# Keeping the intermediate rows of a Fourier mixing kernel in SBUF instead of DRAM, on one Trainium2 core

## The chip, the core and the metric

The kernel runs on one core of one Trainium2 chip. The metric is the device time of one execution in microseconds (us). Every execution quoted here is of the fast state, so no comparison in this document mixes states. The profile is one execution of the same program, with its own span. Engines are called TensorE (PE in the profile, its weight loads PEld), VectorE (DVE), ScalarE (ACT), GpSimd (POOL) and SyncE (SP).

## The reference, cut to what matters

```python
def _attn_ref(x, filt_r, filt_i):                 # x (8, 3136, 256): eight entries
    X = np.fft.rfft(x, axis=1)                    # along the 3136 rows
    Y = X * (filt_r + 1j * filt_i)[None, :, :]
    return np.fft.irfft(Y, n=x.shape[1], axis=1)

def _moe_ref(x, w_in, w_out, g_ln):               # x (25088, 256)
    h = x @ w_in                                  # 256 -> 1024
    e = np.exp(h - max(h));  sm = e / (sum(e) + 1e-09)
    solu = h * sm
    ln = (solu - mean(solu)) / sqrt(var(solu) + 1e-06) * g_ln
    return ln @ w_out                             # 1024 -> 256
```

The transform is done as matrix products of two lengths, 49 and 64 (3136 = 49 x 64): first products `pa` over 49, then per frequency a product `pb` over 64, the filter, the inverse product `pc` over 64, and products `py` back over 49. The second part works in 196 blocks of 128 rows: product `h`, maximum, exponential, normalization, a transposition through SBUF and DMA, product `po`. A block needs the rows of one entry (24.5 blocks each), so the entries 2 to 7 can be transformed beside the blocks of their forerunners.

## The kernel before

Between `pa` and `pb`, and between `pc` and `py`, rows and columns have to change places between partitions. The kernel before does this by a round trip through DRAM each time. Its entries go in groups: entries 0 and 1 together before any block (the prologue), then four groups spread over 150 blocks.

```python
GROUPS = [((0, 1), None, None),                   # prologue
          ((2,), (0, 6), (9, 13)),                # first blocks of pa; of pb/pc
          ((3, 4), (6, 13), (22, 25)),
          ((5, 6), (32, 28), (64, 29)),
          ((7,), (94, 18), (116, 24))]
...
    def store_first(self, i, dma):                # t1 (after pa) -> DRAM
        b, ch = divmod(i, NH // NCH)
        dma(out=d1[self.n][b].rearrange("a (h n) c -> (a h) n c", h=2)[
            :, NCH * ch:NCH * ch + NCH, :], in_=self.t1s.pop(i))

    def fetch(self, i):                           # DRAM -> t2: two DMAs, 64 partitions each
        ...
        for p in range(2):
            nc.sync.dma_start(out=self.t2s[i][N2 * p:N2 * p + N2, 0:cols, :],
                              in_=self.rows(d1[self.n], s, count, p))

    def store(self, i, dma):                      # g (after pc) -> DRAM: two DMAs
        ...
def fetch_back(e, ch, rows_pool):                 # DRAM -> t4, before py
    ...
# in the loop over blocks k:
    hidden(k)          # 8 passes h, 512 columns
    turn(k - 1); regroup(k - 4)       # four DMAs on SyncE
    early jobs         # pa, pb, py of later entries
    project(k - 6)     # 16 passes po, 256 columns
    normalize(k); scale(k - 6)
    products, late jobs, stores, loads
```

The cuts are marked by "..." and by the comments that stand for code.

## Time and profile before

| | before |
|---|---|
| time, median of 3 | 1903.86 us (1903.44 to 1904.51) |
| TensorE busy | 96 % |
| first product `h` in the trace | 203.4 us |
| HBM read, written | 118.44 MB, 81.40 MB |

The chain that ended last follows the work back from the end of the execution. The first line splits it by engine, the second by engine, operation and source line. From the page of the kernel before:

```profile
PE 88%; DVE 4%; DMA 2%; issue 1%; ACT 1%; POOL 0%; ACTq 0%; DVEq 0%; SPq 0%; POOLq 0%
PE h L396 35%; PE po L456 35%; PE py L253 6%; PE pc L226 4%; PE pb L196 4%; PE pa L169 3%; DMA d<-t 1%; DVE p L217 1%; DVE i L216 0%; DVE p L215 0%; DVE g L229 0%; DMA t<-d 0%; DVE nmax L401 0%; DMA f<-f_dram 0%; DMA raw_in<-in_moe_w_in_dram 0%
```

TensorE carries 88 % of the time, 70 % in the two products of the blocks. All round trips through DRAM together hold 1 % of the chain (`d<-t` and `t<-d`), though they are a large part of the 200 MB that pass through HBM: nearly nothing waits for them.

### The profile page before, as it was taken

The page shows a single profiled execution, that of the slowest core. Times are in us where ns is not written, and L with a number is a line of the kernel's source. Part 1 is how long each engine was busy: PE and PEld are TensorE (multiplying, and loading weights), DVE is VectorE, ACT ScalarE, POOL GpSimd, SP SyncE. Part 2 cuts the span into 40 slices and gives each one's busy share as a digit, 9 for nine tenths or more (in the row PEclk, how much of TensorE's full clock was granted, in tenths as well). Part 3 has the DMA queues.
Part 4 walks back from the last instruction along what each step waited for, and adds up shares of the span by engine and source line. Part 5 has one row for each costly group of instructions (what it writes and reads, how often), then busy time and mean ns, then how long its engine had stood idle before and what let it go on. Part 6 is the DMA issues. An engine that isn't in the chain of part 4 may idle for free.

```text
span 1902.9 us, 21234 instructions
## 1 busy us (share of the span) xinstructions
PE 1823.8 (96%) x6500; PEld 1168.5 (61%) x6500; DVE 1137.0 (60%) x1815; ACT 791.5 (42%) x1297; POOL 440.7 (23%) x1293
## 2 busy tenths in 40 slices
PE   6677889999999999999999999999999999999997
PEld 1224546676666666666666666667677676666665
DVE  1597445567766655566766655566666565566663
ACT  1142344554555544444545434344444334333331
POOL 2010133343334311123333211123322010110110
PEclk9686799999999999999999999999999999999999
DMA  9675279986877866575776656557675545434444
GB/s 268 214 211 188 92 226 239 241 209 174 189 194 204 200 150 149 134 170 140 166 186 148 151 137 141 137 134 177 146 178 112 119 100 117 99 86 110 96 92 100
DMA packets 320399, 300.78 MB, mean 158 GB/s; under 512 B 28625, under 2 KB 286418, under 8 KB 320288
## 3 DMA queue, kind: packets, MB, share of 16 engines
q1 hardware_dynamic: 284624, 206.69, 46.3%
q0 software_dynamic: 26704, 79.63, 14.9%
q10 hardware_dynamic: 8960, 13.11, 2.3%
q8 instruction: 53, 0.87, 0.2%
q14 instruction: 58, 0.48, 0.1%
HBM read 118.44 MB, written 81.40 MB: 105 GB/s over the span
## 4 chain that ended last, share of the span: by engine, by line
PE 88%; DVE 4%; DMA 2%; issue 1%; ACT 1%; POOL 0%; ACTq 0%; DVEq 0%; SPq 0%; POOLq 0%
PE h L396 35%; PE po L456 35%; PE py L253 6%; PE pc L226 4%; PE pb L196 4%; PE pa L169 3%; DMA d<-t 1%; DVE p L217 1%; DVE i L216 0%; DVE p L215 0%; DVE g L229 0%; DMA t<-d 0%; DVE nmax L401 0%; DMA f<-f_dram 0%; DMA raw_in<-in_moe_w_in_dram 0%
## 5 line engine op out<-in xcount | busy, mean ns | idle before, releaser
L456 PE MATMUL po<-w_out_sb,solu_t 128*128 128x256 f32 x3136 | 711.0, 380 | 4.5 <-DVE ot L464 4.5
L396 PE MATMUL h<-w_in_sb,y 128*128 128x512 f32 x1568 | 713.4, 598 | 0.0
L456 PEld LDWEIGHTS po<-w_out_sb,solu_t 128*128 128x128 f32 x3136 | 591.0, 190 | 137.7 <-issue 58.1
L396 PEld LDWEIGHTS h<-w_in_sb,y 128*128 128x128 f32 x1568 | 296.2, 192 | 317.8 <-issue 306.7
L401 DVE TENSOR_REDUCE nmax<-h 128x1 f32<-128x1024 f32 x196 | 239.6, 1222 | 419.6 <-PE h L396 419.6
L404 ACT ACTIVATE e<-h,nmax 128x1024 f32<-128x1024 f32 x196 | 218.5, 1115 | 605.0 <-DVE nmax L401 605.0
L421 ACT ACTIVATE e<-solu,nmu 128x1024 f32<-128x1024 f32 x196 | 225.0, 1148 | 287.9 <-DVE solu L419 287.9
L419 DVE SCALAR_TENSOR_TENSOR solu<-e,rsum,h 128x1024 f32<-128x1024 f32 x196 | 250.9, 1280 | 7.1 <-DVE rsum L416 0.2
L429 DVE STREAM_TRANSPOSE turn<-solu 128x1024 f32<-128x1024 f32 x196 | 241.8, 1234 | 0.0
L235 POOL DMA_DIRECT2D d<-g x152 | 93.7, 621 | 507.5 <-ACT g L229 507.4
L253 PEld LDWEIGHTS py<-wi_t,t 100*128 100x128 f32 x1024 | 146.0, 211 | 51.1 <-issue 36.0
L169 PE MATMUL pa<-x,wf_t 98*100 98x512 f32 x256 | 148.5, 687 | 25.9 <-DMA x<-in_x_dram 12.5
L253 PE MATMUL py<-wi_t,t 100*128 100x98 f32 x1024 | 145.4, 293 | 6.7 <-DMA t<-d 3.5
L448 POOL COPY rs_t<-rs 32x1 f32<-32x1 f32 x784 | 141.7, 181 | 35.7
L464 DVE TENSOR_SCALAR ot<-po,rs_t 128x256 f32<-128x256 f32 x196 | 94.4, 482 | 80.5 <-PE po L456 74.2
L215 DVE TENSOR_TENSOR p<-pb,f 128x512 f32<-128x512 f32 (+1 forms) x101 | 69.0, 684 | 120.4 <-ACT i L208 119.3
L196 PE MATMUL pb<-t,de 128*128 128x512 f32 (+1 forms) x250 | 110.9, 544 | 19.2 <-DVE p L215 10.0
L226 PE MATMUL pc<-p,de 128*128 128x512 f32 (+1 forms) x250 | 110.0, 539 | 14.9 <-DVE p L217 11.5
L442 POOL TENSOR_SCALAR rs<-var 128x4 f32<-128x4 f32 x49 | 9.3, 189 | 445.7 <-ACT e L421 443.6
L169 PEld LDWEIGHTS pa<-x,wf_t 98*100 98x100 f32 x256 | 45.7, 188 | 94.5 <-issue 59.9
L196 PEld LDWEIGHTS pb<-t,de 128*128 128x128 f32 x250 | 47.8, 198 | 78.4 <-issue 43.5
L256 ACT COPY y<-py 128x392 f32<-128x392 f32 x112 | 93.6, 836 | 5.1 <-PE py L253 5.1
(62 smaller groups left out, 868.2 us busy)
## 6 DMA issues: line engine op xcount, KB each, us to landing
solu_t<-turn SPq DMA_DIRECT2D x784, 128.0 KB
t<-d SPq DMA_DIRECT2D x64, 400.0 KB
t<-d SPq DMA_DIRECT2D x198, 128.0 KB
x<-in_x_dram SPq DMA_DIRECT2D x64, 392.0 KB
out_dram<-ot SPq DMA_DIRECT2D x196, 128.0 KB
d<-t POOLq DMA_DIRECT2D x48, 400.0 KB, 5.6
d<-g POOLq DMA_DIRECT2D x148, 128.0 KB, 3.6
f<-f_dram POOLq DMA_DIRECT2D x104, 128.0 KB, 4.3
```

What stands on the lines that cost most here:

```text
L169: nc.tensor.matmul(out=ps[0:NK, j], lhsT=wf_t, rhs=self.xs[i][0:NR, 2 * u:2 * u + 2, :], start=True, stop=True)
L196: nc.tensor.matmul(out=ps[:, w * j:w * j + w, :], lhsT=de[:, s + j, 0, :], rhs=t2[:, w * j:w * j + w, :], start=True, stop=True)
L226: nc.tensor.matmul(out=ps[:, w * j:w * j + w, :], lhsT=de[:, s + j, 1, :], rhs=pt[:, w * j:w * j + w, :], start=True, stop=True)
L253: nc.tensor.matmul(out=psv[:, i, :], lhsT=t4s[e, ch][:, i, cb * P:cb * P + P], rhs=wi_t, start=True, stop=True)
L396: nc.tensor.matmul(out=h[:, half, :], lhsT=y[:, c, P * t:P * t + P], rhs=w_in_sb[:, c, 512 * half:512 * half + 512], start=(c == 0), stop= ...
L401: nc.vector.tensor_reduce(out=nmax, in_=h, axis=AX.X, op=ALU.max, negate=True)
L404: nc.scalar.activation(out=e, in_=h, func=AFT.Exp, bias=nmax, accum_out=esum)
L419: nc.vector.scalar_tensor_tensor(out=solu, in0=e, scalar=rsum, in1=hs.pop(k), op0=ALU.mult, op1=ALU.mult, accum_out=nmu)
L421: nc.scalar.activation(out=e, in_=solu, func=AFT.Square, bias=nmu, scale=-float(DFF), accum_out=variances[g][:, i:i + 1])
L429: nc.vector.transpose(out=turns[g][:, :, i, :], in_=solus.pop(k).rearrange("p (f j) -> p f j", j=32))
L448: nc.gpsimd.tensor_copy(out=rss[g][32 * i:32 * i + 32, c:c + 1], in_=rs[32 * c:32 * c + 32, i:i + 1])
L456: nc.tensor.matmul(out=ps, lhsT=solu_t[:, f, :], rhs=w_out_sb[:, f, :], start=(f == 0), stop=(f == KF - 1))
```

## The change

Its intent is to drop the round trips. After `pa` the rows of one entry lie in one SBUF tile, `rows` (100 partitions x 32 x 256). A frequency is then one partition of it, 32 KB, and has to be spread over 32 partitions for `pb`; after `pc` the 32 partitions are gathered into the one, in place. Each such move is one DMA of 32 KB: four of each kind for one column of the transform, eight each way for a unit of two. Because there is one tile, the entries can only follow one another: entry 0 alone before the blocks, entry e beside the 24.5 blocks of entry e-1. To make room, the eviction buffer `g` has one buffer beside the blocks instead of two.

```diff
-    d1 = [dram.tile([len(g[0]), 2 * NS, N2, C], FP32, ...) for n, g in enumerate(GROUPS)]
-    d2 = [dram.tile([len(g[0]), 2 * NS, N2, C], FP32, ...) for n, g in enumerate(GROUPS)]
+    rows = consts.tile([P, NH, C], FP32, name="rows")
 ...
+        def first(self, i, kind, evac):
+            ps = psum(kind, f"pa_{self.e}_{i}")
+            nc.tensor.matmul(out=ps[0:NK], lhsT=wf_t, rhs=self.xs.pop(i)[0:NR], ...)
+            evac(out=rows[0:NK, 2 * i:2 * i + 2, :], in_=ps[0:NK])
+
+        def fetch(self, i):
+            for j in range(count):
+                for a in range(4):
+                    r = NS * a + s + j
+                    nc.sync.dma_start(out=self.t2s[i][NH * a:NH * a + NH, j, :], in_=rows[r:r + 1])
 ...
+        def store(self, i, dmas):
+            for j in range(count):
+                for a in range(4):
+                    r = NS * a + s + j
+                    dmas[a](out=rows[r:r + 1], in_=gt[NH * a:NH * a + NH, j, :])
+
+        def back(self, i, kind, evac):            # py reads rows directly
 ...
-        for name, bufs in (("r", 4), ("t1", 2), ("t2", 3), ("p", 2), ("g", 2))}
+        for name, bufs in (("r", 5), ("i", 1), ("p", 2), ("g", 1))}
 ...
+    for e in range(1, B):
+        base = S * (e - 1) // P
+        pa   at blocks base      to base + 4
+        pb   at blocks base + 6  to base + 18, one unit a block; pc one block later
+        py   at blocks base + 20 to base + 23
```

The last four lines stand for the longer code of the schedule. Weights are unpacked elsewhere in the prologue, and the filter is copied once and saved to DRAM from SBUF.

> **What bounds the kernel now.** I read the page's busy shares first, then its 40 slices, then the stage table, because an average over stages hides where the change acts. On the page, the busy shares, the slices and the costliest groups:
>
> ```profile
> PE 1823.8 (96%) x6500; PEld 1168.5 (61%) x6500; DVE 1137.0 (60%) x1815; ACT 791.5 (42%) x1297; POOL 440.7 (23%) x1293
> ...
> PE   6677889999999999999999999999999999999997
> ...
> DVE  1597445567766655566766655566666565566663
> ...
> PEclk9686799999999999999999999999999999999999
> DMA  9675279986877866575776656557675545434444
> ...
> L456 PE MATMUL po<-w_out_sb,solu_t 128*128 128x256 f32 x3136 | 711.0, 380 | 4.5 <-DVE ot L464 4.5
> L396 PE MATMUL h<-w_in_sb,y 128*128 128x512 f32 x1568 | 713.4, 598 | 0.0
> ```
>
> The reader sees two kernels in one. In the first five slices (47.6 us each) TensorE is busy 6 to 8 tenths and its clock is 0.6 to 0.9; after that TensorE is full. The stage table (time, TensorE, weight load, VectorE, ScalarE, GpSimd busy, granted clock, DMA share, GB/s) says the same in numbers:
>
> ```profile
> 100.00:150.00 50.00, 36.00 (x62) 11.30 (x62) 47.72 (x82) 21.06 (x36) 3.60 (x6) 0.90 0.67 195
> 150.00:200.00 50.00, 38.19 (x136) 29.39 (x137) 30.25 (x60) 10.51 (x15) 2.14 (x3) 0.60 0.49 161
> ...
> 400.00:600.00 200.00, 200.00 (x721) 128.49 (x720) 131.80 (x208) 101.42 (x169) 69.77 (x176) 1.00 0.78 192
> ```
>
> From 100 to 150 us VectorE is the bound (47.7 of 50). From 400 us TensorE is busy for every microsecond at clock 1.00 and VectorE has a third to spare. The timeline shows the first block matmul (h) at 203.4 us. So the kernel is a **prologue** of 204 us (entries 0 and 1 through the transform, weights unpacked, nothing else for TensorE) and a **block stage** of 1699 us (196 blocks of h and po, the other six entries beside them).
>
> What does a unit of TensorE work cost? A busy duration is not it, since matmuls overlap. The chain of waits between 389 and 404 us, where nothing waits, gives it:
>
> ```profile
> 391.49 0.87 PE py L253 x8
> ...
> 397.56 0.95 PE py L253 x8
> 398.51 3.46 PE h L396 x8
> 401.97 0.86 PE pb L196 x4
> 402.83 0.86 PE pa L169 x2
> 403.69 3.45 PE po L456 x16
> ```
>
> So a pass of 512 columns takes 0.43 us, one of 256 columns 0.216, one py pass 0.109. Check: between 500 and 1700 us the trace has 1140 h, 2272 po, 96 pa, 88 + 50 pc, 86 + 50 pb (512 and 256 columns) and 736 py passes: 490.2 + 490.8 + 41.3 + 48.6 + 47.8 + 80.2 = 1198.9 of 1200 us. The block stage runs at the array's rate.
>
> **What the Trainium skill says.** (1) "TensorE: Matmul & The Clock Gate", Part 1 (The HAM clock gate): the array runs at half clock until it has been busy for some 3.4 us. The prologue's 0.60 to 0.90 against 1.00 later agrees. A prologue made of waits is paid twice. (2) "DMA: Bandwidth & Descriptors", Issuing engines are not separate DMA queues: transfers from all issuers share 16 engines, and several issuers save issue time only. Here an issue on SyncE or ScalarE costs 0.28 to 0.62 us (medians 0.28 for a store of t1 on ScalarE, 0.43 for an output, 0.62 for a 64-partition load), one on GpSimd 0.61. (3) "SBUF — State Buffer", Door 1 (The DMA port swizzle): four partitions share a port and reached 27.6 GB/s alone. A 32 KB row sits in one partition, so an estimate from that page is 32.8 KB / 27.6 GB/s = 1.2 us per row move unless rows on different ports overlap. No transfer of the kernel before has this shape, so nothing in its trace tests it.
>
> **The change part by part.** The intermediate goes from two DRAM round trips to one resident tile, rows. Each row (one frequency, 32 x 256) is moved from its partition to 32 partitions by one DMA, and put back by another: 200 row moves of 32 KB per entry. Entry 0 alone is in the prologue; entries 1 to 7 each take the 24.5 blocks before they are needed.
>
> *Block stage, TensorE.* One entry needs 32 pa passes (13.8), 100 pb/pc passes of 256 columns (21.6) and 128 py passes (14.0): 49.3 us. Before: 196 x (8 x 0.43 + 16 x 0.216) = 1351.6, plus 6 x 49.3 = 295.8, sum 1647; the stage took 1699, so 52 us are lost. The table's idle and the tail (1850 to 1903 us holds 42.9 busy of 53) put about 10 at the end, and some 42 between 204 and 400, where the clock is 0.76 and 0.86 at first and the chain waits for DMA d<-t and f<-f_dram. After: 1351.6 + 7 x 49.3 + 3.5 (ps_mean moves here) = **1700 us**. So the seventh entry costs 49 us in the stage that was full. Weight loads grow (800 instead of 500 for pb and pc) but at 256 columns they hide, as they do for po.
>
> *Prologue.* It halves in work, and what bounds it changes. The first landing is at 5.4 us in the trace. x of one entry (3.2 MB) with the tables and two raw weights queued beside it (3.6 MB) at the 250 GB/s or so of the first slices: about 28 us. Then VectorE: one unit is three operations started every 0.605 us (1.8); a weight unpacking is ten operations of 0.42 or 0.69, some 5.1 us in a row; a filter copy is 2 x 0.95. Before the first product stand two unpackings and two copies (14 us), partly under the x load, and the first row needs about 6 us of issue and landing: first product near 40 us. The 13 units with two unpackings and three copies make 23.6 + 10.2 + 5.7 = 40 us on VectorE. SyncE issues ten row moves per unit: at 0.3 us that is 39 us for 13 units, at 0.6 it is 78. I take 45 to 50 for the phase, so its products end near 88. Last inverse, put-back and landing: 5 to 6 us. The 16 back pieces are 14 us at full clock, some 18 with a cold start, beside four unpackings (20 us) on VectorE. Blocks start near **115 us** by this (88 + 6 + 18 = 112, and 3 for what queues behind the tables) instead of 204.
>
> *Startup and tail.* Blocks 0 to 4 now have 2.75 us of pa beside 3.44 of h, so TensorE is less empty than before; but entry 1's x may land only after the pools of the prologue are free, behind the 3.3 MB that saves the filters. I take 15 us of losses instead of 42, partly for the seven seams between entries (pb of the first unit two blocks after its rows are fetched). The tail is untouched: 10 us.
>
> *Beside it.* A unit block has 8.6 us of TensorE work. VectorE needs 4.7 + 2.05, GpSimd eight put-backs at 0.61 plus two filter loads (1.2) and 1.1 of scale work, 7.2; SyncE eight row fetches, four regroups at 0.62 and its share of output, 5.3 at 0.3 us per row and 7.7 at 0.6. All fit, GpSimd and SyncE narrowly. DRAM traffic falls.
>
> Sum: 115 + 1700 + 15 + 10 = **1840 us**, 3.4% less. The gain is the prologue's 89 and about 27 of startup, less 49 + 3.5 of added matmul.
>
> **The rivals.** *A: row moves serialize on the port.* At 1.2 us each, 16 per unit block are 19 us against 8.6 of TensorE, some 10 us x 13 x 7 = 900 us more; at an effective 0.6 us, with other traffic, 1 to 3 us a block and 100 to 250 us more: 1950 or worse. For it: the page's port figure. Against it: the four rows of one frequency lie 25 partitions apart, in different ports, and transfers overlap; the code has been arranged around eight row moves per block, which somebody would not keep at such a price. *B: SyncE or the outstanding transfers bound the prologue.* Issue at 0.6 us, or every DMA waiting for the eighth before it on its semaphore at 4 us under load, makes the unit phase 70 us: 1865 in all. *C: VectorE is late.* Unpacking of w_out stands ahead of the first maximum; if the raw words come late, blocks start 10 us later: 1850. *D: seams.* If SyncE or GpSimd runs behind, a regroup queues behind eight fetches that wait for a row, and po waits: 5 us x 7 entries, 1870. *E: the transfers were hidden anyway.* True from 400 us on, so the DRAM savings are worth nothing there; I give them no time.
>
> **Range and chances.** Start of blocks between 98 and 145 us, startup and seams between 8 and 35, give 1816 to 1890; 8 in 10 falls in 1815 to 1882. The 2% mark is 1866. Faster 0.77; the same 0.14 (B and D together); slower 0.09 (A).
>
> **What would show it.** The first h in the timeline, at 115 us by me. In the stage table, 200.0 of 200 TensorE at clock 1.00 through the middle; less, with a wait of pb for row fetches, is A or D. The idle of py before its first piece tells the put-back. SyncE's issue durations decide 0.3 against 0.6. From first h to the end I expect about 1725 us. The prediction is wrong most likely if row moves are slower than every transfer that the trace shows.

## The result

| | before | after |
|---|---|---|
| time, median of 4 | 1904.18 us (1903.44 to 1904.84) | 2067.31 us (2061.34 to 2074.40) |
| ratio of fast runs, 95 % interval | | 1.0858 (1.0813 to 1.0903) |
| HBM read, written | 118.44, 81.40 MB | 82.40, 28.97 MB |
| first `h` | 203.4 us | 187.2 us |

The changed kernel is correct, moves 88 MB less through HBM, and is 8.6 % slower. Ratios here and below are the mean time of one kernel's fast runs over the mean of the other's fast runs of the same rounds, so not quite the ratio of the medians.

The page of the changed kernel: busy shares, two rows of the 40 slices (51.8 us each), the chain by engine and by line, and groups (busy us, mean ns of one | idle time before them and what ended most of it).

```profile
PE 1878.0 (91%) x6800; PEld 1254.7 (61%) x6800; DVE 1114.2 (54%) x1787; ACT 824.7 (40%) x1354; POOL 700.6 (34%) x1853
...
PE   6549899899989999899999999799998999999998
...
PEclk9966999899999999899999999999999999999999
...
PE 52%; DMA 21%; SPq 9%; issue 8%; POOL 5%; DVE 2%; ACT 2%; POOLq 0%; DVEq 0%; ACTq 0%
...
L206 POOL DMA_DIRECT2D rows<-g x750 | 376.5, 505 | 351.3 <-ACT g L198 304.6
...
L174 PE MATMUL pb<-r_t,de 128*128 128x256 f32 x400 | 130.4, 435 | 96.0 <-DMA r_t<-rows 44.2
L214 PE MATMUL py<-wi_t,rows 100*128 100x98 f32 x1024 | 151.2, 315 | 49.3 <-DMA rows<-g 49.3
...
L198 ACT COPY g<-pc 128x512 f32<-128x512 f32 (+1 forms) x104 | 59.2, 569 | 255.1 <-DMA rows<-g 171.9
```

TensorE fell from 96 to 91 % busy and from 88 to 52 % of the chain. In its place stand DMA (21 %), SyncE's issues (SPq, 9 %) and GpSimd (5 %). TensorE's row has 8s and one 7 among the 9s behind the prologue, where the kernel before had only 9s until its last slice. The group lines name the waits: the evictions of `pc` (`g<-pc`) waited 171.9 us for put-backs (`rows<-g`) to land, `py` 49.3 us for the same, `pb` 44.2 us for row fetches. A wait of ScalarE for a put-back is by itself harmless; it delays the next `pc` and whatever stands behind the eviction in ScalarE's queue. Which wait of TensorE each delay ends in, the trace doesn't tell one by one: behind the first `h`, TensorE waited 40.0 us with `py` for put-backs, 22.2 with `pb` for row fetches, 16.1 with `pb` for the filter products, 14.2 with `pa` for rows of x and 8.3 with `po`.

The stage table of the changed kernel (stretch, its length, busy time of TensorE, weight loads, VectorE, ScalarE, GpSimd, granted TensorE clock, DMA share, GB/s):

```profile
50.00:100.00 50.00, 24.44 (x48) 13.90 (x48) 18.21 (x28) 9.63 (x17) 12.99 (x22) 1.00 0.67 98
100.00:150.00 50.00, 23.08 (x52) 14.24 (x52) 28.25 (x49) 12.54 (x23) 18.73 (x35) 0.65 0.54 78
150.00:200.00 50.00, 46.69 (x174) 36.73 (x175) 21.36 (x45) 20.86 (x29) 1.67 (x3) 0.63 0.49 138
400.00:600.00 200.00, 192.78 (x686) 126.21 (x686) 117.68 (x187) 85.29 (x144) 82.59 (x211) 0.99 0.74 145
1000.00:1200.00 200.00, 186.23 (x696) 126.17 (x695) 102.96 (x162) 82.89 (x136) 68.53 (x185) 0.96 0.67 129
```

From 50 to 150 us no engine is busy for more than 28 of 50 us, and 78 to 98 GB/s flow where the kernel before had 195 to 212: none of these engines is the bound by its busy time. SyncE is not in the table, since issuing a DMA doesn't count as busy: by the durations of its issues it spent 72 % of these 100 us issuing (31 % in the kernel before). The clock of 1.00 from 50 to 100 us is no measurement, since the profile's clock records begin at 98 us; at 86 us a pass of 256 columns took 0.43 us, twice the 0.216 of later ones. From 1000 to 1200 TensorE has 186 of 200 us, with a clock of 0.96, where it had 200 of 200 at 1.00.

**The balance.** I split both traces into three parts: the time to the first `h`; the TensorE work behind it, each pass priced at its undisturbed step (0.43 us for 512 columns, 0.216 for 256, 0.109 for `py`, as the prediction read them); and the rest of the time to the last product, which I call losses. Both end some 5.6 us after the last product.

| us, from the trace | first `h` | TensorE work behind it | losses |
|---|---|---|---|
| before | 203.4 | 1661.9 | 31.9 |
| after | 187.2 | 1696.8 | 181.6 |
| difference | -16.2 | +34.9 | +149.7 |
| the prediction's difference | -89 | +53 | -27 |

The sum of the differences is 168 us, as is the difference of the two spans (2071.1 and 1902.9). Two terms went wrong, the prologue by 73 us and the losses by 177.

**The circle in the prologue.** Timeline of SyncE's queue, after:

```profile
92.30 6.51 SPq L164 DMA_DIRECT2D r_t<-rows  x8
98.91 1.17 SPq L206 DMA_DIRECT2D rows<-g  x2
```

One unit costs SyncE eight fetches in 6.51 us and two of its eight put-backs in 1.17 (in the prologue GpSimd issues four and ScalarE two), 7.7 in all; one of these eight fetches lasted 1.94 us. Over the prologue the fetches start every 0.634 us in the median. Thirteen units took from 52 to 148 us, 7.4 each. From the chain of waits of the same kernel, the end of the prologue:

```profile
149.72 3.29 DMA rows<-g
153.01 0.30 issue
153.31 27.59 PE py L214 x128
180.91 6.41 PE pa L154 x8
187.32 3.43 PE h L393 x8
```

The back transform waits for the last put-back to land, and then takes 27.59 us, 0.216 a pass, twice the 0.109 of later passes: the granted clock is 0.50.

**The circle in the blocks.** Timelines of GpSimd and then of ScalarE in one stretch of a unit phase (start us, us, engine, line, operation, count, and the idle time before with what ended it):

```profile
833.25 3.99 POOL L206 DMA_DIRECT2D rows<-g  x8 [2.82 <-ACT g L198]
841.66 3.96 POOL L206 DMA_DIRECT2D rows<-g  x8 [4.42 <-ACT g L198]
```

```profile
832.38 0.58 ACT L198 COPY g<-pc 128x512 f32<-128x512 f32 x1 [2.47 <-DMA rows<-g]
840.79 0.58 ACT L198 COPY g<-pc 128x512 f32<-128x512 f32 x1 [2.58 <-DMA rows<-g]
```

ScalarE evicts a `pc` at 832.38, GpSimd issues its eight put-backs from 833.25 to 837.24, and ScalarE, idle for 2.58 us, begins the next eviction at 840.79, when the last of them has landed: `g` has one buffer. Over all unit phases the medians of one round are 0.58 us for the eviction, 0.29 to the first issue, 4.02 for eight issues, 3.77 from there to the last landing and 0.22 to the next eviction, 8.9 in all; the median from one eviction to the next is 9.16, the mean 9.71. A unit block has 8.6 us of TensorE work. In 54 of 84 rounds the next eviction began within 0.3 us of the last landing. The seam between two entries, in TensorE's timeline:

```profile
846.31 3.62 PE L453 MATMUL po<-w_out_sb,solu_t 128*128 128x256 f32 x16
856.13 5.41 PE L214 MATMUL py<-wi_t,rows 100*128 100x98 f32 x24 [6.21 <-DMA rows<-g]
```

TensorE stands still for 6.21 us until the last put-back of the entry has landed. The seams between entries cost 41 us in all, and passes of `py` and `po` that waited for nothing lost another 34 to a lower granted clock.

### The profile page after: what moved, and what is told of

The parts are those of the page before. It is cut to its first block, busy times and chain, and to the rows that moved or that the text cites. A ratio compares the mean times of both kernels' runs of the same rounds, so it can differ in the third digit from the quotient of the medians.

```text
span 2071.1 us, 24728 instructions
## 1 busy us (share of the span) xinstructions
PE 1878.0 (91%) x6800; PEld 1254.7 (61%) x6800; DVE 1114.2 (54%) x1787; ACT 824.7 (40%) x1354; POOL 700.6 (34%) x1853
## 3 DMA queue, kind: packets, MB, share of 16 engines
HBM read 82.40 MB, written 28.97 MB: 54 GB/s over the span
## 4 chain that ended last, share of the span: by engine, by line
PE 52%; DMA 21%; SPq 9%; issue 8%; POOL 5%; DVE 2%; ACT 2%; POOLq 0%; DVEq 0%; ACTq 0%
PE po L453 20%; PE h L393 18%; PE py L214 7%; DMA rows<-g 6%; DMA solu_t<-turn 5%; SPq L164 5%; DMA r_t<-rows 5%; PE pa L154 4%; POOL rows L206 4%; DMA r_x<-in_x_dram 4%; SPq L435 3%; PE pb L174 1%; DMA out_dram<-ot 1%; PE pc L195 1%; SPq L466 1%
## 5 line engine op out<-in xcount | busy, mean ns | idle before, releaser
L453 PE MATMUL po<-w_out_sb,solu_t 128*128 128x256 f32 x3136 | 726.4, 386 | 8.3 <-DVE ot L461 8.3
L453 PEld LDWEIGHTS po<-w_out_sb,solu_t 128*128 128x128 f32 x3136 | 605.4, 194 | 131.2 <-issue 35.0
L206 POOL DMA_DIRECT2D rows<-g x750 | 376.5, 505 | 351.3 <-ACT g L198 304.6
L174 PE MATMUL pb<-r_t,de 128*128 128x256 f32 x400 | 130.4, 435 | 96.0 <-DMA r_t<-rows 44.2
L214 PE MATMUL py<-wi_t,rows 100*128 100x98 f32 x1024 | 151.2, 315 | 49.3 <-DMA rows<-g 49.3
L214 PEld LDWEIGHTS py<-wi_t,rows 100*128 100x128 f32 x1024 | 150.3, 230 | 63.7 <-issue 49.2
L174 PEld LDWEIGHTS pb<-r_t,de 128*128 128x128 f32 x400 | 73.4, 205 | 180.3 <-issue 131.5
L154 PE MATMUL pa<-r_x,wf_t 98*100 98x512 f32 x256 | 142.2, 672 | 29.8 <-DMA r_x<-in_x_dram 28.9
L198 ACT COPY g<-pc 128x512 f32<-128x512 f32 (+1 forms) x104 | 59.2, 569 | 255.1 <-DMA rows<-g 171.9
L381 POOL DMA_DIRECT2D f<-f_dram x182 | 94.6, 525 | 181.6 <-DVE i L187 128.3
```

Source lines behind the costliest of these rows:

```text
L154: nc.tensor.matmul(out=ps[0:NK], lhsT=wf_t, rhs=self.xs.pop(i)[0:NR], start=True, stop=True)
L174: nc.tensor.matmul(out=ps[:, j, :], lhsT=de[:, s + j, 0, :], rhs=t2[:, j, :], start=True, stop=True)
L206: dmas[a](out=rows[r:r + 1], in_=gt[NH * a:NH * a + NH, j, :])
L214: nc.tensor.matmul(out=psv[:, j, :], lhsT=rows[0:NK, 4 * n + j, cb * P:cb * P + P], rhs=wi_t, start=True, stop=True)
L453: nc.tensor.matmul(out=ps, lhsT=solu_t[:, f, :], rhs=w_out_sb[:, f, :], start=(f == 0), stop=(f == KF - 1))
```

## The experiments

The questions were: are the row moves slow because a row lies in one partition (P, the port); because there are so many issues on SyncE (S); because the put-backs go round with one buffer (G); or does the order of entries lose by itself (O)? Kernels said to be wrong give a wrong result on purpose. Times are medians; the kernel before had 1904 to 1908 us in the same rounds.

### One fetch per row, but from a table (control): getrow, wrong

```diff
 def fetch(self, i):
+    if self.e:       # source: one partition of the constant table, 32 rows by a broadcast
+        nc.sync.dma_start(out=self.t2s[i][NH*a:NH*a+NH, j, :], in_=de[r:r+1, s, :, :] ... broadcast)
```

> Control of the run before: eight fetches per unit, each reading 32 KB from one partition of the constant table (wrong result on purpose). It differs from the changed kernel only in that a fetch no longer waits for the rows of its own entry. All theories expect no more than 20 to 30 us off 2067; what it gains is the price of the fetch waiting for the first transform at each entry's start.

Measured: 2068.33 us, ratio 1.0844 (1.0822 to 1.0865); losses 171 us. It equals the changed kernel, so the fetches' dependence on the first transform costs nothing, and the two runs below can be compared with it.

### The same eight fetches from 32 partitions each: get32, wrong

```diff
+    nc.sync.dma_start(out=self.t2s[i][NH*a:NH*a+NH, j, :], in_=de[NH*a:NH*a+NH, s + j, :, :])
```

> The row fetches stay eight per unit and 32 KB each, but each reads 32 partitions of a constant table instead of one partition (wrong result on purpose). S expects the time of the next run (eight fetches from one partition of the same table) within 15 us, since the number of issues is the same. P expects it 40 us or more faster than the next run. G expects both the same as the changed kernel, 2067, within 20.

Measured: 2104.62 us, ratio 1.1029 (1.1006 to 1.1053). With a source spread over 32 partitions it is slower, not faster. So P, the rival that I feared most, falls for the fetches. For put-backs into one partition no run here tells it. The median landing of the put-backs rose from 4.0 (getrow) to 4.8 us, and the time rose with it: the first sign that the put-backs carry the time.

### One fetch of 256 KB per unit instead of eight of 32: flatget, wrong

```diff
+    nc.sync.dma_start(out=self.t2s[i][:, 0:count, :], in_=de[:, s:s + count, :, :] ...)
```

> For entries 1 to 7 the eight row fetches of a unit (32 KB each) become one transfer of the same 256 KB, from 128 partitions of a constant table (wrong result on purpose). S (SyncE's issues bound a unit block: 8 x 0.63 + 4 x 0.70 + 0.75 = 9.2 us against 8.6 of TensorE) expects SyncE at about 5 us per unit block and 60 to 100 us off the changed kernel's 2067, to about 1985. G (the put-back chain bounds it: one g buffer, 4.0 us of GpSimd issue, then some 4 us to landing, then the next eviction) expects at most 20 us off. P (one partition's port serializes the row moves) expects some 40 to 80 off, since half of the row moves go.

Measured: 2086.84 us, ratio 1.0941 (1.0919 to 1.0964). SyncE lost seven of its eight fetch issues per unit, and the kernel got some 20 us slower (18.5 against the control getrow of the same rounds). S alone is not the bound. The put-backs landed in 4.44 us instead of 4.19, and the evictions waited 218 us for them instead of 172.

### The order alone, with the DRAM round trips of before: neworder, correct

```diff
-GROUPS = [((0, 1), None, None), ((2,), (0, 6), (9, 13)), ((3, 4), (6, 13), (22, 25)), ...]
+STARTS = [0, 0] + [S * (e - 1) // P - 10 for e in range(2, B)]
+GROUPS = [((0,), None, None)] + [
+    ((e,), (STARTS[e], 5), (STARTS[e] + (6 if e == 1 else 8), 13)) for e in range(1, B)]
 ...      # the blocks of py and how early rows are loaded follow
```

From entry 2 on, this schedule starts `pa` ten blocks and `pb` eight blocks earlier than the changed kernel does: it is the one-by-one order, but not block for block the changed kernel's.

> One part alone: the kernel before, its DRAM round trips and its few large transfers, but one entry in the prologue and entries 1 to 7 one after another beside the blocks (correct result). If the row moves are what costs (S, G or P), TensorE is full from the first blocks on, the prologue ends near 130 to 145 us and the total is 1700 + 140 + 25 + 10, about 1875, faster than both kernels. If the order itself costs (an entry's stages too dense for 24.5 blocks), it is at 1950 or above like the changed kernel.

Measured: 1957.06 us, ratio 1.0262 (1.0244 to 1.0280). First `h` at 161.9 us, 41.5 earlier than before; work behind it +36; losses 90 instead of 32. So this order costs 49 us against the kernel before in the same rounds (52 between the profiled spans) without any row move: halving the entries of the prologue doesn't halve its time, and what moves into the blocks is paid in full. Its stage table, two stretches:

```profile
350.00:400.00 50.00, 36.04 (x139) 25.52 (x138) 18.15 (x30) 14.40 (x23) 9.39 (x27) 0.83 0.58 131
...
600.00:800.00 200.00, 200.00 (x777) 138.56 (x776) 121.42 (x194) 92.55 (x152) 58.70 (x165) 0.99 0.71 174
```

Between 600 and 800 us it loses nothing; entry 1, started late and squeezed beside the first blocks, loses up to 14 of 50 us at 350 to 400.

### Two buffers for the evicted rows: g2, correct

```diff
-    ones = consts.tile(...); w_bar = consts.tile(...)      # moved into a spare buffer of g, for room
-    (("r", NB), ("i", 1), ("p", 2), ("g", 1))
+    (("r", NB), ("i", 1), ("p", 2), ("g", 2))
```

> The changed kernel with two g buffers instead of one (the two small constants of the weight preparation lie in that pool, for space; correct result). G (one put-back must land before the next eviction, and ScalarE stands still meanwhile: 172 us of its waits) expects ScalarE's wait on put-backs to fall below 60 us and 30 to 90 us off the changed kernel's 2067. S (SyncE's 9.2 us of issues per unit block) expects less than 15 us off, since SyncE's queue is as long as before. Both together in series: 15 to 40 off now, the rest in the next run but one.

Measured: 2027.39 us, ratio 1.0633 (1.0599 to 1.0667), losses 140. G is real: one more buffer gives 40 us. What is left has changed its name. The waits of TensorE in this run (total us, times, longest):

```profile
PE pb L172 <- DMA r_t<-rows: 69.6, 41, 5.6
...
PE py L212 <- DMA rows<-g: 20.1, 5, 12.4
```

`py`'s wait fell from 49.3 to 20.1 us, and `pb`'s wait for row fetches rose from 44.2 to 69.6. SyncE's steps in the block stage say why: eight fetches at 0.73 us, four regroups at 0.71 and its share of output at about 0.5 make 9.2 us per unit block, against 8.6 of TensorE. These are steps from start to start and hold waits: the issues themselves fill 76 % of SyncE's time in the unit phases of g2.

### Both at once: flatget_g2, wrong

The edits of flatget and g2 together.

> Two g buffers and one row fetch per unit from a constant table instead of eight (wrong result on purpose). If S and G are two queues of nearly the same length that hide each other, this is the first run that gains much: unit blocks at TensorE's 8.6 us, losses of the block stage from 182 to about 80 (the seven seams with their 40 us stay), 1950 to 1980 in all. If G alone counts, it equals the run with two g buffers within 15.

Measured: 1978.72 us, ratio 1.0387 (1.0356 to 1.0418), losses 85.

| us | eight fetches | one fetch |
|---|---|---|
| one `g` buffer | 2067 | 2087 |
| two `g` buffers | 2027 | 1979 |

This square is the main finding. Fewer fetches cost 20 us with one buffer and give 48 with two. Two bounds stand one behind the other: the put-backs' round first, the eight fetches on SyncE second. Whether these bind by SyncE's time per issue, by the places for transfers under way (see proget2 below) or by their landing is not separated: one large fetch takes away all three.

### Half of the put-backs: halfput, wrong

```diff
 def store(self, i, dmas):
-    for j in range(count):
+    for j in range(1 if self.e else count):
```

> Entries 1 to 7 put back only the first row of each unit's two: four put-backs per unit instead of eight (wrong result on purpose), one g buffer as in the changed kernel. GpSimd's issue per unit falls from 4.0 to 2.0 us. G expects as much as or more than from the second buffer, 30 to 90 us off 2067, and a shorter wait before the back transform at the seams. S expects less than 15 off.

Measured: 1963.77 us, ratio 1.0292 (1.0241 to 1.0343), losses 68. With four put-backs per unit, landing in 3.3 us, the last landing comes 2.9 us before the next eviction in the median, and a unit block takes 8.73 us, TensorE's own time, though all fetches are there and `g` has one buffer. Fewer put-backs also relieve the fetches: their mean step fell from 0.735 to 0.664 us. So each transfer got cheaper when fewer were under way.

### Half of the prologue's fetches issued by ScalarE: proget2, correct

```diff
+    dma = nc.scalar.dma_start if self.e == 0 and a % 2 else nc.sync.dma_start
```

> In the prologue only, half of the row fetches are issued by ScalarE instead of SyncE (correct result): SyncE then issues six transfers per unit instead of ten, at 0.63 us each 3.8 us instead of 6.3. S for the prologue expects the 13 units to take 65 to 80 us instead of 96 and the first block matmul near 165 instead of 187: 15 to 30 us off 2067. If the landing of the row moves or VectorE bounds the prologue, less than 8 us off.

Measured: 2081.56 us, ratio 1.0928 (1.0898 to 1.0959), first `h` at 190.8 us. No gain. The timelines of SyncE's and of ScalarE's queue in this run, one unit:

```profile
93.33 4.69 SPq L165 DMA_DIRECT2D r_t<-rows  x4
...
93.47 4.83 ACTq L165 DMA_DIRECT2D r_t<-rows  x4
```

Each row covers four fetches and a wait of some 2.4 us in the middle. An issue itself lasted no longer than before: 0.56 us on SyncE and 0.57 on ScalarE in the mean, against 0.60. What SyncE waited for from 47 to 132 us (total us, times, longest), first in the changed kernel, then in this one:

```profile
SPq L164 <- DMA rows<-g: 1.2, 2, 0.7
...
SPq L165 <- DMA rows<-g: 19.1, 12, 3.0
```

A fetch doesn't need the put-back that it waits for. The semaphores in the trace tell why it waits: in these programs the transfers of SyncE and ScalarE take turns on eight common semaphores, and none begins before the one that had its semaphore before has landed. So at no time in either trace are more than eight of them under way. In the changed kernel 11 of SyncE's 118 row moves in that stretch began within 0.1 us of such a landing; here it was 25 of 67, and 33 of ScalarE's 67, and a row move took 3.8 us to land instead of 3.2. So the second issuer took SyncE's issues from 83 to 44 % of its time and met the next bound, eight transfers under way, which the prediction's rival B named. "Perfetto Trace Analysis", DMA Optimizations, advises to balance transfers over the issuing engines where descriptor generation is the bottleneck; here that gave nothing.

### Half of the row moves in the prologue: prohalf, wrong

```diff
-    for j in range(count):          # in fetch and in store
+    for j in range(count if self.e else 1):
     # pb of entry 0 reads the one column that was fetched, twice
```

> In the prologue only, entry 0 moves just the first row of each unit's two, out and back: 100 row moves instead of 200 (wrong result on purpose). If the row moves bound the prologue's units, by SyncE's 0.63 us per issue (ten per unit) or by the eight transfers that may be out at once (2.7 to 5 us each to landing), the 13 units take 48 to 60 us instead of 96 and the first block matmul comes near 145 instead of 187: 35 to 50 us off 2067. If VectorE's unpacking bounds them (40 us of work in that phase by the prediction), 10 us off at most.

Measured: 2028.98 us, ratio 1.0641 (1.0604 to 1.0679). First `h` at 147.6 us, 39.6 earlier; losses 178, unchanged. The row moves bound the units of the prologue: the last `pc` ends at 106.3 us instead of 144.1.

### Dense products among the back transforms of the prologue: warmback, correct

```diff
+        warm = ps_h.tile([P, 2, 512], FP32, name="warm", tag="h")
         for i in range(en.parts):
             en.back(i, "tbto"[i % 4], nc.scalar.copy)
+            nc.tensor.matmul(out=warm[:, 0, 0:256], lhsT=de[:, 0, 0, :], rhs=de[:, 0:2, 0, :],
+                             start=True, stop=True)       # never read
```

> In the prologue's back transform one dense 128x128 by 256 product, unused, follows each of the 16 pieces (correct result; 32 passes, 7 us at full clock). The back pieces now run 27.6 us at half clock though TensorE never pauses. If the narrow passes (98 columns of 100 rows) are too thin to release the clock and a dense one is enough, py passes fall to 0.109 us and the first block matmul comes 8 to 15 us earlier. If the clock needs only time, or a longer dense stretch, the added products cost 7 to 14 us and it comes later.

Measured: 2066.81 us, ratio 1.0833 (1.0783 to 1.0882): the time is that of the changed kernel. In the profiles the first `h` comes at 182.9 us instead of 187.2, though TensorE has about 7 us more to do. Stage tables, first the changed kernel, then this one:

```profile
165.00:180.00 15.00, 15.00 (x72) 15.00 (x72) 5.61 (x11) 7.49 (x9) 0.00 (x0) 0.50 0.32 91
180.00:187.00 7.00, 7.00 (x13) 2.98 (x13) 0.00 (x0) 2.66 (x5) 0.00 (x0) 0.52 0.21 60
```

```profile
155.00:165.00 10.00, 9.56 (x52) 9.08 (x53) 3.56 (x8) 3.75 (x5) 0.72 (x1) 0.70 1.00 288
165.00:185.00 20.00, 20.00 (x124) 16.17 (x123) 7.61 (x15) 12.26 (x16) 0.00 (x0) 1.00 0.49 139
```

In the changed kernel TensorE is busy without a pause from 153 to 187 us, and the clock stays at 0.50. With one dense 128 x 128 x 256 product after every eight narrow passes it is 0.70 over the first 10 us and 1.00 from then on; in the trace of that run the change comes 5.7 us after the first back piece. In all 14 traces without such products, the kernel before among them, the clock of these back pieces is 0.50. The step of 18 us in the prediction failed for that reason. The first `h` gained less than the 8 to 15 us that were expected. The 4 us are less than the spread of the runs (2057.0 to 2076.5).

### Two attempts at the prologue of the DRAM path: before2 and neworder2, correct

before2 is the kernel before with the unpacking of `w_out` moved in among the back transforms; neworder2 is neworder with that and with two frequencies per unit.

> The kernel before with the unpacking of w_out put after the back transform's loads in program order, so that VectorE does part of it beside the py passes, with all py evictions on ScalarE and two raw buffers (correct result). VectorE bounds the prologue from 72 to 140 us in the kernel before; 20 us of unpacking leave it. Expected: first block matmul at 185 to 198 instead of 203, 1885 to 1900 in all.

> The new order on the old path, with its prologue shortened: units of two rows (15 products of up to 512 columns instead of 25 of 256) and the unpacking of w_out beside the back transform (correct result). VectorE's work in the unit phase falls by some 12 + 20 us. Expected: first block matmul near 135 instead of 162, total 1925 to 1935 against 1957. It passes the kernel before only if the prologue falls to about 110.

Measured: before2 1904.19 us, ratio 0.9977 (0.9953 to 1.0001), first `h` at 204.8: no gain. neworder2 1950.07 us, ratio 1.0222 (1.0195 to 1.0250), first `h` at 159.7 instead of 161.9: a miss, as before2 is. My reading that VectorE's unpackings bind the DRAM path's prologue earns next to nothing, but it is not refuted: from 100 to 150 us VectorE was busy for 48.6 of 50 us in before2, as for 47.7 in the kernel before, so the edit didn't take its work out of that stretch. What binds a single entry's way through the stages I leave open.

### Half of all row moves and two buffers: halfall_g2, wrong

The loops of prohalf without the condition on the entry, and the buffers of g2.

> The changed kernel with half of the row moves in every entry, out and back, and two buffers for the evicted rows; wrong result on purpose. Theory M (the row moves, by their issues on SyncE and their put-back chain, make nearly all of the loss): first h near 147 us as with half moves in the prologue alone, losses of the block stage 65 to 85 us, time 1900 to 1930 us, so about the kernel before's 1907. Theory O (the order of blocks and entries loses by itself, whatever the row moves cost): block-stage losses stay above 120 us and the time above 1960 us.

Measured: 1924.52 us, ratio 1.0100 (1.0078 to 1.0121). First `h` at 146.2 us, losses 73. The chain by engine, and a stretch of the stage table:

```profile
PE 79%; DMA 8%; issue 5%; POOL 2%; DVE 2%; SPq 2%; ACT 1%; POOLq 0%; ACTq 0%; DVEq 0%
```

```profile
400.00:600.00 200.00, 198.88 (x780) 136.47 (x779) 120.68 (x193) 93.55 (x154) 57.70 (x164) 1.00 0.67 136
```

With half of the row moves, 143 of the 163 us are gone, prologue and blocks together: the row moves, with the one buffer behind them, carry the loss. But even then the kernel is 1 % slower than before (within the 2 % called the same). The start is 57 us earlier than before, 35 us of work come in behind it, and the losses are 41 higher than before's 32. The largest single wait of TensorE behind the first `h` is now `pa` for rows of x, 13.2 us; the changed kernel has 14.2 of it, g2 13.5 and halfput 15.4.

### The clock in the kernel before: before_warm, correct

```diff
+            warm = ps_h.tile([P, 2, 512], FP32, name="warm", tag="h")
+            for ch in range(6): fetch_back(0, ch, pools["r"])      # loads, six ahead
+            for _ in range(5): dense(4)              # 128x128x512, ahead of the back transforms
             for ch in range(NH // NCH):             # the later loads stand here, cut
                 for cb in range(KD):
                     back(0, ch, cb, either)
+                    dense(2)                         # 128x128x256 after each
```

> The kernel before with dense products added among the back transforms of the prologue, so that TensorE's clock is granted in full there; correct result. If the half clock of that stretch is time on the path, the first h comes earlier and the time falls by 5 to 12 us (0.3 to 0.6 %). If the stretch is bound by its loads and the evictions, or the added products cost what the clock gives, the time stays within 3 us of 1907.

Measured over five rounds: 1899.98 us (1897.07 to 1903.72), before 1905.70 (1901.92 to 1910.78), ratio 0.9968 (0.9951 to 0.9986). It is the fastest kernel of the study, by 0.3 %, which is far within the 2 % called the same. The clock did what was wanted. Stage tables, the kernel before, then this one:

```profile
200.00:210.00 10.00, 10.00 (x30) 6.52 (x30) 4.29 (x8) 1.22 (x2) 0.00 (x0) 0.61 0.01 2
```

```profile
200.00:210.00 10.00, 10.00 (x75) 9.55 (x74) 5.64 (x10) 2.92 (x4) 0.00 (x0) 1.00 0.01 2
```

But the first `h` came at 210.8 us, not earlier than 203.4, and the losses behind it were 24.4 instead of 31.9. The size was as expected and the way was not: at the first `h` nothing is gained, and the smaller losses come behind it. That the blocks gain because they begin with a full clock is argued; the edit also moves six loads ahead and fixes the order of the stage, so the 6 us are not the clock's alone. The profiled run was the slowest of its six, so I don't split them further.

## Why the prediction was wrong, point by point

**What was right.** The kernel before was read rightly as bound by TensorE, with its DRAM traffic hidden, and rival E was right: saving 88 MB gave nothing. The TensorE work of the changed block stage, 1700 us, came out as 1696.8 (passes counted in the trace, at the prediction's prices). The doubts named SyncE's issue (rival B), the seams (D) and, as its most likely failure, row moves slower than the transfers of the trace; B is what happened in the prologue, far larger than the few us given to it. D named the right place and not the right wait (below). The reading that VectorE bounds the old prologue from 100 to 150 us was not tested by before2 or neworder2.

**The prologue, 115 us by the prediction, 187.2 in the trace.** Terms (1), (2) and (4) failed, by about 48, 12 and 16 us; (3) held only in part. (1) "SyncE issues ten row moves per unit: at 0.3 us that is 39 us for 13 units, at 0.6 it is 78. I take 45 to 50 for the phase": it took 96. The fetches start every 0.634 us, so even the worse figure was short, and proget2 shows that a second issuing engine doesn't help while both share eight places for transfers. The figure of 0.3 came from a store of t1 on ScalarE, a transfer of another shape. prohalf confirms the term: half of the moves, 39.6 us less. (2) The last rows of x landed at 45 us and the first product of a unit came at 52.5; the estimates were 28 and 40. (3) "Last inverse, put-back and landing: 5 to 6 us": from the last eviction on it is 4.8 us (148.56 to 153.31), but the last inverse product had ended at 144.1, and its eviction waited for an earlier put-back; I count that wait to the phase in (1). (4) "The 16 back pieces are 14 us at full clock, some 18 with a cold start": 27.59, and 6.4 more for `pa` that now comes ahead of `h`, all at clock 0.50.

**The work behind, +53 by the prediction, +34.9.** The 1647 us for the kernel before left out the `py` of entry 1, 128 passes x 0.109 = 14.0, which stand in its block stage. The balance closed all the same, because I called the missing 15 us losses. So I saw 52 us of losses and tail where there are 32 and 6; the other 14 were work, which the hoped-for gain of 27 us could not come from.

**The losses, 15 + 10 by the prediction, 181.6.** The step that failed is "All fit, GpSimd and SyncE narrowly". I summed each engine's time per block: GpSimd 7.2, SyncE 7.7 at most. Such sums were the wrong measure. GpSimd's time was if anything put too high (0.50 us per put-back instead of 0.61), but with one `g` buffer eviction, issues and landing go round in 8.9 us, and 9.7 in the mean with what comes between. I had the line `g` 2 to 1 in the diff before me and gave it no sentence. Behind it stood SyncE with 9.2 us per unit block, waits included, instead of 5.3 to 7.7. g2, flatget and flatget_g2 show both and their order. "5 us x 7 entries" of rival D (1875 in all, not 1870) met the 41 us at the seams in size, but by luck: D had `po` wait for a regroup behind eight fetches, and in the trace `py` waits for the last put-back, 40.0 us in seven waits, while no wait of `po` for a regroup over 0.15 us appears. The 34 us of lower clock the prediction left out.

**Rival A, the port.** It got the slow chance. Its figure of "1950 or worse" is what came, but not for its reason where that was tested: for the fetches get32 was slower than getrow. Sixteen moves at 1.2 us in series would make 19 us, and the mean round of the put-backs is 9.7, so that price is refuted for both. A smaller share of the port in the put-backs stays open.

**The order.** The prediction gave the order a gain of 36 us (89 - 53). neworder measures its own version of it at 49 us of loss: a prologue of one entry is 41.5 us shorter, not 89, since the stages that an entry passes through don't halve, and entry 1 is squeezed beside the first blocks. Of the 150 us of added losses, 58 appear in neworder already. The other 92 can't simply be put down to the row moves: halfall_g2, in the changed kernel's order, has 73 us of losses in all, fewer than neworder's 90, so part of the 58 belongs to neworder's own schedule.

**What stays open.** Which property of the eight fetches on SyncE makes the second bound; why the put-backs' landing grows when fetches get bigger or broader; what the order costs with the row moves' own schedule; and what binds the prologue of neworder2.

## What to carry to other kernels

Ask of every transfer that you remove whether anything waited for it; here 1 % of the chain did, so 88 MB less were worth nothing. Price a buffer that is cut from two to one as a round (issue, landing, eviction) and not as a sum of busy times: the round is the bound if it is longer than the block. And when two bounds may stand in series, try both cures together as well as singly, since one alone can look harmful. Before issues are spread over engines, see how many transfers may be under way at once: in proget2 the second issuer only met that limit.

## What the Trainium skill lacked or had wrong

- "TensorE: Matmul & The Clock Gate", Part 1 (The HAM clock gate), says that some 3.4 us of sustained activity release the clock. Here TensorE was busy without a pause for 34 us (153 to 187) at clock 0.50, mostly in passes of 98 columns on 100 rows; with a dense 128 x 128 x 256 product after every eight of them it was 1.00 some 6 us after the start. In 14 traces without such products these back pieces ran at 0.50. The page doesn't say that being busy with narrow passes isn't enough.
- "DMA: Bandwidth & Descriptors", Issuing engines are not separate DMA queues, says that several issuers save only the time to initiate a DMA, which is usually small beside the DMA itself. For 32 KB row moves it was 0.634 us from start to start against 3.2 us to land in the prologue: small for one, but eight in a row made 5 to 6.5 us of a unit's 7.4. No page tells of the limit of eight transfers under way that these programs put on SyncE and ScalarE together, and that took the gain in proget2.
- "SBUF — State Buffer", Door 1 (The DMA port swizzle), gives one port 27.6 GB/s and 32 partitions 189. Eight concurrent fetches of 32 KB from single partitions were no slower than from 32 partitions (2068 against 2105 us for the kernel); for these transfers the port figures did not tell which is faster.
- "SBUF — State Buffer", The DMA setup-cost knee, has about 2 us of fixed cost and a fit that makes 2.1 us of 32 KB. The put-backs took 4.2 us in the median with eight of them and eight fetches per block under way, and 3.3 us with half as many put-backs.
- No page tells how long a put-back from 32 partitions into one takes, the shape that bound this kernel.
